# Holding back the loads of the key weights in a fused attention and MLP kernel until an earlier load has landed

## The chip, the cores and the metric

The kernel runs on one core of a Trainium2 chip. The metric is the device time of one execution in microseconds (us). The core has five instruction streams that matter here: TensorE (matrix products, PE in the profile, with its weight loads as PEld), VectorE (DVE), ScalarE (ACT), GpSimd (POOL) and SyncE (SP). SyncE, ScalarE and GpSimd also issue transfers (DMAs) between the chip's memory and the core's own memory. Issued transfers are carried out by 16 DMA engines; the profile calls SyncE's issues SPq and ScalarE's ACTq.

## The reference

One input x of 2048 tokens by 640 features goes through a linear attention block (A) and a gated MLP mixer block (B); a sigmoid gate per token mixes the two results. Only what matters for the change is shown.

```python
def _A_ref(x, wqkv, wo):
    B, S, D = x.shape              # 1, 2048, 640
    H = 32; Dh = D // H
    qkv = (x @ wqkv).reshape(B, S, 3, H, Dh).transpose(2, 0, 3, 1, 4)
    q, k, v = qkv[0], qkv[1], qkv[2]
    phi = lambda t: jnp.where(t > 0, t + 1, jnp.exp(t)) + 1e-6
    pq, pk = phi(q), phi(k)
    kv = jnp.einsum("bhsd,bhse->bhde", pk, v)
    z = jnp.einsum("bhsd->bhd", pk)
    ...
g = _sigmoid((x * gate_w).sum(-1, keepdims=True))
a = _A_ref(x, A_wqkv, A_wo)
b = _B_ref(x, B_w1, B_w2, B_w3, B_w4)
return g * a + (1 - g) * b
```

All inputs are bfloat16. The weight wqkv is 640 by 1920: columns 0 to 639 make the queries, 640 to 1279 the keys, 1280 to 1919 the values.

## The kernel before

The tokens are cut into 16 tiles of 128. x tile t is loaded as 128 rows of 640 values (160 KB) into x_tok. The products need x with features along the partitions, so each tile is also turned into xT: tiles 0 to 2 by TensorE (t_x, five transposes of 128x128 against an identity matrix, then copies by VectorE), tiles 3 to 15 by a transposing DMA (x_turn). The feature dimension of 640 is cut into five blocks k of 128. Query weights are loaded as five slices wq0 to wq4 of 128 rows by 512 columns (128 KB each) and one tail of the last 128 columns of all rows (160 KB, called wqt); key weights as five slices wk0 to wk4 of 128 rows by 640 columns (160 KB each) into wkg.

The order of work around the change is fixed by the order of the calls. The loads are issued in the order of lines 714 to 739:

| queue | order of issue |
|---|---|
| SyncE | x0, x1, wq2, x2, wk0, wk2, x3, wk4, x4, turn of x3, x5, turn of x4, tiles 6 to 9, turns of 5 to 7, tiles 10 to 15, turns of 8 to 15 |
| ScalarE | wq0, wq1, wq3, wq4, wk1, wk3, tail of wq; then the load of ScalarE's function table, and the exponentials |

A queue carries out its own instructions in order, so a wait on it holds everything behind it. Each transfer has a semaphore of its own; whoever reads its result waits for that. The helper sch.dma takes a list deps of events to wait for ahead of the issue, and keeps the event of the last transfer under each name in sch.dma_last.

TensorE begins with products on constants that only keep it busy (warmup), and then goes through q_three (line 949): the query products of token tiles 0 to 2, one per tile and block k, in a hand-written order in which the transposes of a tile are (t, None):

```python
order = [(0, 0), (1, None), (0, 1), (1, 0), (1, 1), (0, 2), (1, 2), (0, 3), (1, 3), (2, None), (0, 4), (1, 4),
         (2, 0), (2, 1), (2, 2), (2, 3), (2, 4)]
```

The transposes of tile 0 precede it. So the transposes of x tile 2 stand behind (1, 3), and the first product behind them, (0, 4), reads wq4. Then k_two (line 958) makes the key products of tiles 0 and 1, each a pair of 512 and 130 columns (line 942 and line 614 of the helper mm_kept), in this order:

```python
stream([(0, 0), (0, 1), (1, 0), (0, 2), (1, 1), (0, 3), (1, 2), (0, 4), (1, 3), (1, 4)], wkg, 130, k_out)
```

so wk0 is read first, wk1 second, wk2 fourth, wk3 sixth and wk4 eighth. The key products of tile 2 follow (k_tile, line 819), then for each further tile the query products (q_tile, line 920, helper line 606) and the key products; tile 3 is the first that reads a turned xT from a DMA. phi (line 809) turns each product into the attention's feature: an exponential on ScalarE (line 682) and two operations on VectorE. Everything later (the Gram matrix of keys and x, the MLP, the output) follows on TensorE with no change of order.

The order of the later items is chosen at build time by a list scheduler (_Items.run) with a cost model; the loads of lines 714 to 739 are issued ahead of it.

Of the kernel before, what the change touches and what calls it, by code (L numbers as in the profile page):

```python
# [11 lines left out]
D = 640  # L12
# [404 lines left out]
def _build(nc, A_x, A_wqkv, A_wo, B_w1, B_w2, B_w3, B_w4, gate_w, out, dbg=None, stop=None):  # L417
    sch = _Sched(nc)
# [80 lines left out]
    wkg = ra.alloc("wkg", [128, KD, NK], BF16)  # L499
# [206 lines left out]
        sch.dma(queue, wq[:, k, 0:512], A_wqkv[128 * k:128 * (k + 1), 0:512], "wq%d" % k)  # L706

    def load_wk(k, queue):
        sch.dma(queue, wkg[:, k, 0:D], A_wqkv[128 * k:128 * (k + 1), D:2 * D], "wk%d" % k)

    def x_turn(t):
        sch.dma("sp", xT[:, :, 128 * t:128 * (t + 1)], x_tok[:, t, :], "trx%d" % (t % 4), transpose=True)
# [9 lines left out]
    load_x(2)  # L722
    load_wq(4, "act")
    load_wk(0, "sp")
    load_wk(1, "act")
    load_wk(2, "sp")
    load_x(3)
    load_wk(3, "act")
# [241 lines left out]
    for i in range(3, NT + 2):  # L970
        if i < NT:
            addA(("q", i), 1.08, lambda t=i: q_tile(t))
            addA(("k", i), 1.36, lambda t=i: k_tile(t))
            if i % 4 == 3:
                addA(("qx", i // 4), 1.08, lambda c=i // 4: q_turned(c))
                IT.add("QB", ("qb", i // 4), 0.0, lambda c=i // 4: q_back(c),
                       deps=[(("qx", i // 4), 2.5), (("t1", NT - 1), 0.0) if i == NT - 1 else (("k", i + 1), 0.0)])
# [380 lines left out]
    for c in range(NCH):  # L1358
        for j in range(KD):
            deps = [(("t1", u), 0.9) for u in range(4 * c, 4 * c + 4)] if j == 0 else []  # L1360
# [7 lines left out]
    for t in range(NT):  # L1368
        c = t // 4
        deps = [(("w1", c, KD - 1), GEL)]  # L1370
# [8 lines left out]
    for u in range(NT):  # L1379
        deps = [(("s2", u // 4), 3.2 + 0.9 * (u % 4))]  # L1380
# [8 lines left out]
    for c in range(NCH):  # L1389
        for j in range(KFF):  # L1390
            deps = []
# [4 lines left out]
            if j == 0:  # L1396
                deps = deps0 + [(("t2", u), 0.9) for u in range(4 * c, 4 * c + 4)]
# [11 lines left out]
    for t in range(NT):  # L1409
        deps = [(("zb",), 1.0), (("q", max(t, 2)), 2.0), (("sg", 1), 0.0)]  # L1410
# [13 lines left out]
    for t in range(NT):  # L1424
# [3 lines left out]
        deps = [(("qt", t), 3.0), (("w4load",), 0.0), (("mt",), 2.5)]  # L1428
# [71 lines left out]
```

## Time and profile before

| | us |
|---|---|
| median of 3 runs | 259.19 |
| lowest and highest run | 259.15, 259.87 |
| span of the profiled execution, first to last instruction | 258.4 |
| mean granted clock of TensorE | 1.000 of full speed |
| first issue of a load (x0, on SyncE) | 0.79 |
| first exponential on ScalarE | 8.71 |

In the profile a row of the timeline has the start in us, the length in us, the engine, the line of the kernel, the operation, what it writes and reads, its shape and how many were merged; in brackets stands how long the engine was idle before it and what ended that. Products on TensorE are pipelined: a busy time of several products can hold gaps between them. The list of DMA issues gives for each group the size and the median time from the issue to the landing; asked for a window that holds one issue, it gives that one transfer's time. The q rows give what each DMA queue moved in a window, in packets, MB and as a share of 16 engines. The table by stages gives for each stretch the busy time of each engine, the granted clock, the busy share of the DMA engines and the rate in GB/s.

### The profile page before, as it was taken

How to read it: one execution, taken by the hardware profiler on the slowest of the kernel's cores; microseconds unless marked ns; L12 is line 12 of the kernel's file. 1: busy time of each engine (PE TensorE's matmuls, PEld its weight loads, DVE VectorE, ACT ScalarE, POOL GpSimd, SP SyncE). 2: the span in 40 equal slices, each digit the busy share in tenths (PEclk: the TensorE clock that was granted, in tenths of full speed). 3: DMA queues.
4: the chain of work that ended last, by engine and by line, in shares of the span. 5: the costliest groups of instructions: out<-in, count | busy, mean ns of one | idle time of the engine just before them, and what ended most of it. 6: DMA issues, size and time to landing. Idle time of an engine off the chain costs nothing.

```text
span 258.4 us, 3579 instructions
## 1 busy us (share of the span) xinstructions
PE 253.2 (98%) x1392; PEld 110.9 (43%) x1242; DVE 145.6 (56%) x290; ACT 107.0 (41%) x219; POOL 90.2 (35%) x146
## 2 busy tenths in 40 slices
PE   8899999999999999999999999999999999999997
PEld 4333333344444333334444444444444444444444
DVE  2588888899962995489999803759200033200033
ACT  1396776751356757665655600003520100253000
POOL 5012299967772143758918001223000022300000
DMA  6777799555843599462565400032100032200002
GB/s 189 221 176 182 155 142 220 157 125 119 111 102 72 103 321 387 95 103 51 127 104 128 102 10 20 0 127 50 28 0 0 20 23 101 101 1 3 0 20 102
DMA packets 57825, 26.48 MB, mean 103 GB/s; under 512 B 49188, under 2 KB 56397, under 8 KB 57808
## 3 DMA queue, kind: packets, MB, share of 16 engines
q1 hardware_dynamic: 54976, 21.87, 36.1%
q0 software_dynamic: 1168, 3.28, 4.9%
q10 hardware_dynamic: 1664, 1.11, 1.4%
q8 instruction: 10, 0.16, 0.3%
q14 instruction: 7, 0.06, 0.1%
HBM read 12.04 MB, written 2.62 MB: 57 GB/s over the span
## 4 chain that ended last, share of the span: by engine, by line
PE 95%; DMA 2%; issue 1%; SPq 0%; DVE 0%
PE ps L606 37%; PE ps L1237 30%; PE ps L625 13%; PE ps L831 7%; PE ps L614 4%; DMA x_tok<-in_A_x_dram 2%; PE ps L942 1%; PE ps L1283 1%; PE ps L1143 1%; SPq L285 0%; PE ps L1029 0%; DVE Mt L691 0%; PE ps L637 0%; PE ps L1055 0%; DVE x_tok L665 0%
## 5 line engine op out<-in xcount | busy, mean ns | idle before, releaser
L606 PE MATMUL ps<-xnT,w 128*128 128x512 bf16 x352 | 79.9, 379 | 0.5 <-issue 0.2
L665 DVE SCALAR_TENSOR_TENSOR x_tok<-ps,stg,abx 128x512 bf16<-128x512 f32 (+2 forms) x17 | 12.2, 719 | 78.4 <-PE ps L1237 78.3
L682 ACT ACTIVATE h2T<-ps 128x512 bf16<-128x512 f32 x52 | 30.7, 596 | 59.8 <-PE ps L606 59.8
L606 PEld LDWEIGHTS ps<-xnT,w 128*128 128x128 bf16 x360 | 34.6, 98 | 41.5 <-issue 2.1
L1237 PE MATMUL ps<-w,h2T 128*128 128x512 bf16 (+2 forms) x218 | 45.9, 366 | 0.3 <-issue 0.2
L648 POOL TENSOR_SCALAR xn<-x_tok,st 128x640 bf16<-128x640 bf16 x32 | 34.2, 1076 | 25.8 <-DMA xnT<-xn 25.3
L648 POOL TENSOR_SCALAR abx<-x_tok,stg 128x640 f32<-128x640 bf16 (+1 forms) x16 | 14.8, 934 | 72.1 <-DVE x_tok L665 72.1
L1237 PEld LDWEIGHTS ps<-w,h2T 128*128 128x128 bf16 x221 | 21.1, 98 | 24.2 <-issue 0.3
L682 ACT ACTIVATE Er<-ps 128x512 bf16<-128x512 f32 (+1 forms) x36 | 23.0, 648 | 15.5 <-PE ps L614 10.6
L681 ACT ACTIVATE junk<-x_tok 128x640 bf16<-128x640 bf16 x32 | 23.6, 738 | 3.9 <-DVE x_tok L663 3.7
L682 ACT ACTIVATE hsT<-ps 128x512 bf16<-128x512 f32 (+1 forms) x32 | 19.0, 593 | 13.5 <-PE ps L606 13.2
L625 PE MATMUL ps<-w,hsT 128*128 128x512 bf16 x76 | 22.3, 379 | 0.0
L625 PE MATMUL ps<-wkg,xT 128*128 128x512 bf16 x67 | 20.1, 379 | 0.1
L663 DVE SCALAR_TENSOR_TENSOR x_tok<-ps,x_tok 128x640 bf16<-128x640 f32 x16 | 13.1, 820 | 10.8 <-PE ps L614 10.2
L1237 PE MATMUL ps<-M_sb,pqnT 128*128 128x512 bf16 (+2 forms) x83 | 18.7, 366 | 0.1
L614 PE MATMUL ps<-wkg,xT 128*128 128x130 bf16 x80 | 17.6, 220 | 0.2
L831 PE MATMUL ps<-pk_tok,x_tok 128*128 128x512 bf16 x79 | 17.7, 379 | 0.1
L614 PE MATMUL ps<-w,hsT 128*128 128x128 bf16 x80 | 17.5, 219 | 0.2
L1172 DVE TENSOR_TENSOR pq_tok<-pq_tok,dnr 128x300 bf16<-128x300 bf16 (+1 forms) x48 | 17.1, 410 | 0.6
L648 DVE TENSOR_SCALAR Er<-Er 128x512 bf16<-128x512 bf16 (+1 forms) x36 | 12.2, 340 | 6.8 <-ACT Er L682 6.0
L606 PE MATMUL ps<-wq,xT 128*128 128x512 bf16 x64 | 15.9, 379 | 0.0
L656 DVE TENSOR_TENSOR qprod<-qprod,pk_tok 128x640 f32<-128x640 f32 x13 | 15.1, 1164 | 0.4
(90 smaller groups left out, 252.8 us busy)
## 6 DMA issues: line engine op xcount, KB each, us to landing
w<-in_B_w_dram SPq DMA_DIRECT2D x1, 2160.0 KB, 8.1
w<-in_B_w_dram SPq DMA_DIRECT2D x1, 2080.0 KB, 13.0
out_dram<-x_tok SPq DMA_DIRECT2D x3, 640.0 KB, 3.1
w<-in_B_w_dram POOLq DMA_DIRECT2D x8, 160.0 KB, 4.0
x_tok<-in_A_x_dram SPq DMA_DIRECT2D x6, 160.0 KB, 4.4
x_tok<-in_A_x_dram SPq DMA_DIRECT2D x1, 960.0 KB, 5.8
wv<-in_A_wqkv_dram POOLq DMA_DIRECT2D x1, 800.0 KB, 5.5
x_tok<-in_A_x_dram SPq DMA_DIRECT2D x1, 640.0 KB, 4.9
```

Source lines behind the costliest of these rows:

```text
L606: ins = e.matmul(out_ap, l, r, start=(i == 0), stop=(i == n - 1))
L614: return e.add_instruction(mybir.InstMatmult(name=nc.get_next_instruction_name(), engine=e.engine, ins=[e.lower_ap(r), ll], outs=[e.lower_ ...
L625: e.matmul(outs[0], l, r, start=st, stop=sp, skip_group_check=True)
L648: return engf(lambda e: e.tensor_scalar(out_ap, in_ap, s1, s2, op0, op1), rd, [out_ap], cost=cost)
L656: return engf(lambda e: e.tensor_tensor(out_ap, a, b_, op), [a, b_], [out_ap], cost=cost)
L663: return dve(lambda e: e.scalar_tensor_tensor(out_ap, in0, scalar, in1, op0, op1, accum_out=accum), rd, [out_ap, accum], cost=cost + 70.0)
L665: return dve(lambda e: e.scalar_tensor_tensor(out_ap, in0, scalar, in1, op0, op1), rd, [out_ap], cost=cost)
L681: return act(lambda e: e.activation(out_ap, in_ap, func, bias=bias, scale=scale, accum_out=accum), rd, wr, cost=cost)
L682: return act(lambda e: e.activation(out_ap, in_ap, func, bias=bias, scale=scale), rd, wr, cost=cost)
L831: ins = e.matmul(o, l, r, start=(t0 + q_ == 0), stop=(t0 + q_ == NT - 1))
L1172: dve(lambda e, o=o, i0=i0, i1=i1: e.tensor_tensor(o, i0, i1, ALU.mult), [i0, dnr[:, 1, sd, :]], [o], cost=cost)
L1237: ins = e.matmul(o, l, r, start=first and i == 0, stop=last and i == len(prs) - 1, skip_group_check=True)
```

## The change

Every key slice's issue gets a dependency: on SyncE's queue the event of x1, on ScalarE's the event of wq1. A queue waits once, ahead of its first key slice (wk0 on SyncE, wk1 on ScalarE); its later key slices find the event passed. What stands behind on the queue follows the wait: on SyncE wk2, x3, wk4, x4 and the turns, on ScalarE wk3, the tail of wq and the load of the function table. No other instruction is added or removed, and the order on every engine stays.

```diff
     def load_wk(k, queue):
-        sch.dma(queue, wkg[:, k, 0:D], A_wqkv[128 * k:128 * (k + 1), D:2 * D], "wk%d" % k)
+        sch.dma(queue, wkg[:, k, 0:D], A_wqkv[128 * k:128 * (k + 1), D:2 * D], "wk%d" % k,
+                deps=[sch.dma_last["x1" if queue == "sp" else "wq1"]])
```

## The prediction

> **What bounds the kernel now.** First the page's head, its busy times and its chain of what ended last:
>
> ```profile
> span 258.4 us, 3579 instructions
> ...
> PE 253.2 (98%) x1392; PEld 110.9 (43%) x1242; DVE 145.6 (56%) x290; ACT 107.0 (41%) x219; POOL 90.2 (35%) x146
> ...
> PE 95%; DMA 2%; issue 1%; SPq 0%; DVE 0%
> ```
>
> TensorE is busy for 253.2 of 258.4 us, and 95% of the chain is its own work. An edit to the loads counts only through the 5.2 us in which TensorE is idle. So the next view is the chain of waits in the first 12 us, the only stretch where a load stands in it:
>
> ```profile
> 1.26 0.41 SPq L285
> ...
> 2.18 5.75 DMA x_tok<-in_A_x_dram
> ...
> 7.98 0.45 PE ps L637 x5
> ...
> 8.44 1.82 PE ps L942 x8
> ```
>
> Columns are start, length and what. The load of x tile 2, issued at 2.18, is on the path until it lands at 7.93; from the transposes of that tile on, every step is TensorE. Time saved or lost before some 14 us therefore passes whole to the end, unless another wait appears. Next the timeline of TensorE there (two views, products and weight loads):
>
> ```profile
> 5.21 2.04 PE L942 MATMUL ps<-wq,xT 128*128 128x512 bf16 x7
> 7.98 0.45 PE L637 MATMUL ps<-ident,x_tok 128*128 128x128 bf16 x5 [0.73 <-DMA x_tok<-in_A_x_dram]
> ...
> 8.30 1.74 PE L942 MATMUL ps<-wq,xT 128*128 128x512 bf16 x7
> 9.88 0.38 PE L942 MATMUL ps<-wkg,xT 128*128 128x512 bf16 x1
> ...
> 10.15 0.38 PE L942 MATMUL ps<-wkg,xT 128*128 128x512 bf16 x1
> ```
>
> ```profile
> 6.21 0.55 PEld L942 LDWEIGHTS ps<-wq,xT 128*128 128x128 bf16 x4 [0.36 <-DMA wq<-in_A_wqkv_dram]
> ```
>
> Two waits for loads: 0.36 us for wq slice 2, then 0.73 us for x tile 2. Together 1.09 us is all that earlier loads can return. The key products start at 9.88 and follow each other every 0.27 us.
>
> **What the change moves.** No instruction is added, removed or reordered on TensorE, VectorE or GpSimd; SyncE and ScalarE each get one wait ahead of their first key slice. Their queues now:
>
> ```profile
> 2.18 0.43 SPq L285 DMA_DIRECT2D x_tok<-in_A_x_dram  x1
> 2.66 0.91 SPq L285 DMA_DIRECT2D wkg<-in_A_wqkv_dram  x2
> 3.61 0.43 SPq L285 DMA_DIRECT2D x_tok<-in_A_x_dram  x1
> 4.08 0.65 SPq L285 DMA_DIRECT2D wkg<-in_A_wqkv_dram  x1
> 4.78 0.69 SPq L285 DMA_DIRECT2D x_tok<-in_A_x_dram  x1
> 10.20 1.29 SPq L281 DMA_TRANSPOSE xT<-x_tok  x1
> ```
>
> ```profile
> 0.80 1.85 ACTq L285 DMA_DIRECT2D wq<-in_A_wqkv_dram  x4
> 2.69 0.94 ACTq L285 DMA_DIRECT2D wkg<-in_A_wqkv_dram  x2
> 3.66 0.46 ACTq L285 DMA_DIRECT2D wq<-in_A_wqkv_dram  x1
> 4.15 1.28 ACT L682 ACT_TABLE_LOAD   x1 [4.15 <-issue]
> 8.71 1.08 ACT L682 ACTIVATE Er<-ps 128x512 bf16<-128x512 f32 x2 [3.28 <-PE ps L942]
> ```
>
> And the time from issue to landing (last column, us), from the list of DMA issues asked for short windows, in this order: x1, wq1, x2, wq4, wk0, wk1, x3, wk4, and last x5, which is issued at 11.54, after all those in this list have landed:
>
> ```profile
> x_tok<-in_A_x_dram SPq DMA_DIRECT2D x1, 160.0 KB, 3.1
> ...
> wq<-in_A_wqkv_dram ACTq DMA_DIRECT2D x1, 128.0 KB, 3.3
> ...
> x_tok<-in_A_x_dram SPq DMA_DIRECT2D x1, 160.0 KB, 5.8
> ...
> wq<-in_A_wqkv_dram ACTq DMA_DIRECT2D x1, 128.0 KB, 5.9
> ...
> wkg<-in_A_wqkv_dram SPq DMA_DIRECT2D x1, 160.0 KB, 6.0
> ...
> wkg<-in_A_wqkv_dram ACTq DMA_DIRECT2D x1, 160.0 KB, 6.2
> ...
> x_tok<-in_A_x_dram SPq DMA_DIRECT2D x1, 160.0 KB, 6.6
> ...
> wkg<-in_A_wqkv_dram SPq DMA_DIRECT2D x1, 160.0 KB, 6.7
> ...
> x_tok<-in_A_x_dram SPq DMA_DIRECT2D x1, 160.0 KB, 2.6
> ```
>
> *SyncE's hold.* x1 lands at 1.26 + 3.1 = 4.36. The hand-over from a landing to a waiting queue is under 0.05 us: x3 lands at 3.61 + 6.6 = 10.2, and the transpose that waits for it starts at 10.20. So wk0 is issued at about 4.4 in place of 2.66, and what is queued behind it (wk2, x3, wk4, x4) shifts by the same 1.75 us, x4's issue ending at 5.47 + 1.75 = 7.2. Then the queue stands still until 10.20 as it does now: 3.0 us of cover.
>
> *ScalarE's hold.* The second of four issues in 1.85 us starts at 0.80 + 0.46 = 1.26; wq1 lands at about 4.6. So wk1 moves from 2.69 to 4.6, by 1.9 us, with wk3, the tail of wq and the table load behind it. The table load then runs from 6.05 to 7.35, ahead of the first exponential at 8.71: 1.35 us of cover, and without that cover it would delay the first exponential only.
>
> *Whether the key slices land later.* Were the queue ahead of them empty, wk0 would land 2.6 us (x5's time) after 4.4, at 7.0, and wk1 at 7.2. Now they land at 2.66 + 6.0 = 8.66 and 2.69 + 6.2 = 8.9. For wk4 the same sum gives 5.83 + 2.6 = 8.4 against 4.08 + 6.7 = 10.8 now, for x3 5.36 + 2.6 = 8.0 against 10.2. Every held transfer is thus issued at least 1.6 us before issuing could limit it: what sets its landing is the work queued ahead. Bounds: 0 at the best, and at the worst every landing moves by the whole shift, priced among the rivals. I take 0, the end that x5's row is nearer to.
>
> *Whether x2 and wq4 land sooner.* The reverse question: did the key slices take anything from them? The two queues' totals from 0 to 6 us (packets, MB, share of 16 engines):
>
> ```profile
> q1 hardware_dynamic: 544, 0.59, 33.1%
> q10 hardware_dynamic: 514, 0.47, 25.5%
> ```
>
> q1 is SyncE's queue, q10 ScalarE's. x0, x1, wq2 and x2 are 608 KB (0.62 MB), the four wq slices of ScalarE 512 KB (0.52 MB). Six microseconds in, neither queue had moved even that much: over the mean of the engines no key slice had begun to flow, though they had been issued for over 3 us. Landings come in the order of issue on each queue. A transfer that waits its turn behind x2 takes nothing from x2. I take 0 gain; the bound is 0.73 + 0.36 = 1.09 us. If x2 alone came sooner, little would follow: wq4, issued at 0.80 + 3 x 0.46 = 2.2, lands at 8.1, and the first product behind the transposes, which reads it, starts at 8.30, so 0.2 us is the most.
>
> *The sum.* 258.4 (span) + 0 (SyncE's hold) + 0 (ScalarE's hold) + 0 (key slices) - 0 (x2 and wq4) = 258.4 us. The runs' median, 259.19, is 0.8 above the profiled span, so 259.2 us.
>
> **The rivals.** *Gain: the queued transfers slow the ones ahead of them.* The DMA rate by stage (last column GB/s, beside it the busy share):
>
> ```profile
> 4.00:6.00 2.00, 2.00 (x14) 1.13 (x12) 1.36 (x5) 1.28 (x1) 0.71 (x5) 1.00 0.77 230
> 6.00:8.00 2.00, 1.20 (x6) 0.33 (x6) 0.00 (x0) 0.00 (x0) 0.00 (x0) 1.00 1.05 368
> ```
>
> Between 4 and 6 us, with wq2, wq3, x2 and wq4 due, the engines are 77% busy and move 230 GB/s, later 368. If the issuing and queueing of eight more transfers causes that dip, holding them lifts it: the 460 KB of that stage at 368 GB/s take 1.25 us, so x2 lands 0.75 us sooner, at 7.18, and wq4 at 7.35. The transposes then start when the products before them end, at 5.21 + 2.04 = 7.25, 0.73 us sooner; with wq2's wait gone too, up to 1.09. Time: about 258.4. For it: the dip has no other cause in these rows, and x5 alone lands in 2.6 where x2 took 5.8. Against it: most of x2's 5.8 is its turn behind x0, x1 and wq2, and both x2 and wq4 must gain. The Trainium skill, "DMA: Bandwidth & Descriptors", section "Latency and other measured facts", says that a lighter HBM load makes the fixed part of a transfer smaller; by that rule too the time would be this rival's. The trace agrees that a lone transfer is quicker, 2.6 against 5.8, but not that load beyond the turn is the reason.
>
> *Loss: late issue shows in the key products.* If the landing times are bound to the issue after all, wk0 lands at 8.66 + 1.75 = 10.4 against 9.88 (0.53 late), wk1 at 8.9 + 1.9 = 10.8 against 10.15 (0.65), wk4 at 10.8 + 1.75 = 12.5 against the eighth key product at 9.88 + 7 x 0.27 = 11.8 (0.75). These run one behind the other, so the largest counts: 0.75 us, 259.95 us. It decides from a shift of 1.0 us on, wk4's margin. x3 would then land at 11.95 and its transpose 2.5 us later, at 14.5, inside the delayed 13.96 + 0.75 = 14.7 of the product that reads it, and adds nothing:
>
> ```profile
> xT<-x_tok SPq DMA_TRANSPOSE x1, 2.5
> ...
> 13.96 1.24 PE L606 MATMUL ps<-wq,xT 128*128 128x512 bf16 x5
> ```
>
> For it: the hold is real, 1.75 us. Against it: x5's row. The Trainium skill's rule on the same page, section "Rules for kernel authors", speaks against the change as well: issue early and wait late, so that the fixed cost is overlapped. By that rule the sum would be this rival's 259.95.
>
> *The wait holds nothing.* If x1 had landed when the queue came to the wait, all would stay at 259.2. The rows exclude it almost: the queue arrives at 2.66, x1 at 4.36.
>
> **How the numbers follow.** No change 0.56 (own range 258.9 to 259.5); gain 0.24, of which I put 0.16 beyond 0.78 us, since that needs wq2's wait too or a still larger lift; loss 0.18, of which 0.13 beyond 0.78, its price of 0.75 standing at that edge and any wait that I have not seen adding to it; the idle wait 0.02. With 0.3% (0.78 us) as about what a measurement of this kernel can tell from no change: faster 0.16, same 0.71, slower 0.13. The range 258.3 to 260.0 takes in the gain up to 0.9 us and the loss up to 0.8, and leaves out the last 0.2 us of the gain's bound and losses past the priced one: under 2 in 10.
>
> **What would show it.** Right: wk0's issue at 4.4 and wk1's at 4.6, the table load ended before 7.5, x2's landing within 0.2 us of 7.93, wk4's within 0.5 us of 10.8, TensorE's wait for x tile 2 still near 0.7 and no wait for wkg. The gain: x2 and wq4 landing near 7.2, the transposes at 7.25, a rate near 368 GB/s already between 4 and 6 us. The loss: a TensorE or weight-load wait for wkg around 10 to 12 us. I am wrong if the two queues do not keep the order of issue, or if the rate after 6 us falls because the held transfers are issued only then.

## The result and the profile after

| | before | changed |
|---|---|---|
| median of 22 runs each, us | 259.08 | 259.72 |
| lowest and highest run, us | 258.18, 260.11 | 258.57, 260.41 |
| span of the profiled execution, us | 258.4 | 258.6 |

The ratio of the changed kernel to the one before is 1.0022, with a 95% interval of 1.0012 to 1.0032: 0.6 us slower, real, but under the 0.3% that the prediction takes for no change. The forecast was 259.2 us in a range of 258.3 to 260.0. The measured time lies in that range, 0.5 us above the forecast, outside the 258.9 to 259.5 that belonged to no change, and nearer to the 259.95 of the rival for the loss. That it is this near is luck: things that the forecast had put at nothing have opposite signs and nearly the same size. The page of the changed kernel, its head, busy times and the chain of what ended last by engine:

```profile
span 258.6 us, 3605 instructions
...
PE 254.8 (99%) x1418; PEld 111.0 (43%) x1242; DVE 146.3 (57%) x290; ACT 107.1 (41%) x219; POOL 90.3 (35%) x146
...
PE 91%; DMA 7%; SPq 1%; DVE 0%; issue 0%
```

Two things are to be seen. TensorE's count went from 1392 to 1418 although the change adds no product: records of products can be missing from a trace, so neither count nor busy time is compared. And transfers, which held 2% of the chain, hold 7%. The chain of the changed kernel, from its start, tells which (start, length, what):

```profile
1.25 2.92 DMA x_tok<-in_A_x_dram
...
4.19 0.33 SPq L285
...
5.04 5.54 DMA x_tok<-in_A_x_dram
...
10.59 1.29 SPq L281
...
11.93 2.66 DMA x_tok<-in_A_x_dram
...
14.61 6.26 DMA xT<-x_tok
...
20.91 1.25 PE ps L606 x5
```

Before, the chain left the loads at 7.98 us, with the transposes of x tile 2, and was TensorE from there on. Now it runs through SyncE's queue up to 20.91: x1's landing releases the held queue (4.19), x3 is loaded (5.04 to 10.58), then turned, then x5 lands, and the turn of tile 5, issued at 14.61, lands only 6.26 us later. The query products of tile 5 wait for it. TensorE's timeline there, changed kernel (products; then the weight load of the transposes of tile 2, before and changed; then products again):

```profile
5.21 1.86 PE L943 MATMUL ps<-wq,xT 128*128 128x512 bf16 x7
6.91 0.44 PE L637 MATMUL ps<-ident,x_tok 128*128 128x128 bf16 x5
...
8.79 0.38 PE L943 MATMUL ps<-wkg,xT 128*128 128x512 bf16 x1
...
9.47 0.39 PE L943 MATMUL ps<-wkg,xT 128*128 128x512 bf16 x1 [0.24 <-DMA wkg<-in_A_wqkv_dram]
```

```profile
7.98 0.28 PEld L637 LDWEIGHTS ps<-ident,x_tok 128*128 128x128 bf16 x5 [1.22 <-DMA x_tok<-in_A_x_dram]
```

```profile
6.84 0.33 PEld L637 LDWEIGHTS ps<-ident,x_tok 128*128 128x128 bf16 x5 [0.27 <-DMA x_tok<-in_A_x_dram]
```

```profile
13.35 1.24 PE L606 MATMUL ps<-wq,xT 128*128 128x512 bf16 x5
...
20.91 1.25 PE L606 MATMUL ps<-wq,xT 128*128 128x512 bf16 x5 [0.62 <-DMA xT<-x_tok]
```

The products no longer stand idle for x tile 2, and the weight loads wait less: 0.27 us for x tile 2 in place of 1.22, 0.18 us for wq slice 2 in place of 0.36. The transposes of tile 2 start at 6.91 in place of 7.98, the key products at 8.79 in place of 9.88. The second key product, which reads wk1, then waits for its load. The query products of tile 3 start at 13.35 against 13.96, and those of tile 5 at 20.91 against 20.74: the lead is used up between tiles 3 and 5. The two held queues and some of their landings (the last column is us from issue to landing; in order x2, wq4, wk0, wk1, wk4, turn of tile 5):

```profile
4.19 0.80 SPq L285 DMA_DIRECT2D wkg<-in_A_wqkv_dram  x2
...
14.61 1.21 SPq L281 DMA_TRANSPOSE xT<-x_tok  x1
```

```profile
4.49 0.85 ACTq L285 DMA_DIRECT2D wkg<-in_A_wqkv_dram  x2
...
5.86 1.28 ACT L682 ACT_TABLE_LOAD   x1 [5.86 <-issue]
7.63 1.08 ACT L682 ACTIVATE Er<-ps 128x512 bf16<-128x512 f32 x2 [0.48 <-PE ps L943]
```

```profile
x_tok<-in_A_x_dram SPq DMA_DIRECT2D x1, 160.0 KB, 4.6
...
wq<-in_A_wqkv_dram ACTq DMA_DIRECT2D x1, 128.0 KB, 4.8
...
wkg<-in_A_wqkv_dram SPq DMA_DIRECT2D x1, 160.0 KB, 3.9
...
wkg<-in_A_wqkv_dram ACTq DMA_DIRECT2D x1, 160.0 KB, 4.9
...
wkg<-in_A_wqkv_dram SPq DMA_DIRECT2D x1, 160.0 KB, 5.6
...
xT<-x_tok SPq DMA_TRANSPOSE x1, 6.3
```

x2 took 5.8 before and takes 4.6, wq4 5.9 and now 4.8. The first exponential still waits for TensorE, not for the table load that ends ahead of it. The table by stages (busy time of PE, PEld, DVE, ACT and POOL with their counts, granted clock, busy share of the DMA engines, GB/s) shows the dip between 4 and 6 us, 230 GB/s before, at 292, and between 6 and 8 us 282, where it was 368:

```profile
4.00:6.00 2.00, 2.00 (x14) 1.11 (x12) 1.36 (x5) 0.14 (x1) 0.73 (x5) 1.00 0.98 292
6.00:8.00 2.00, 2.00 (x15) 0.97 (x15) 0.58 (x4) 1.52 (x2) 0.00 (x0) 1.00 0.88 282
```

One thing about the profile before has to be known for all that follows: x2 came late in it. Two further profiles of the same kernel (under the experiments) have spans of 257.8 us in place of 258.4. In all runs where time and span are of the same execution, the time is 1.2 to 1.3 us above the span; the 0.8 of the prediction compared one execution's span with the median of others.

### The profile page after: what moved, and what is told of

The parts are those of the page before. It is cut to its first block, busy times and chain, and to the rows that moved or that the text cites. A ratio compares the mean times of both kernels' runs of the same rounds, so it can differ in the third digit from the quotient of the medians.

```text
span 258.6 us, 3605 instructions
## 1 busy us (share of the span) xinstructions
PE 254.8 (99%) x1418; PEld 111.0 (43%) x1242; DVE 146.3 (57%) x290; ACT 107.1 (41%) x219; POOL 90.3 (35%) x146
## 4 chain that ended last, share of the span: by engine, by line
PE 91%; DMA 7%; SPq 1%; DVE 0%; issue 0%
PE ps L606 36%; PE ps L1238 30%; PE ps L625 12%; PE ps L832 7%; DMA x_tok<-in_A_x_dram 4%; PE ps L614 3%; DMA xT<-x_tok 2%; PE ps L1284 1%; PE ps L1144 1%; SPq L281 0%; SPq L285 0%; PE ps L1030 0%; DVE Mt L691 0%; PE ps L1056 0%; DVE x_tok L665 0%
## 5 line engine op out<-in xcount | busy, mean ns | idle before, releaser
L625 PE MATMUL ps<-w,hsT 128*128 128x512 bf16 x80 | 23.0, 379 | 0.0
```

The costliest lines, as they stand in the source:

```text
L625: e.matmul(outs[0], l, r, start=st, stop=sp, skip_group_check=True)
```

## The experiments

Every row of the table is one execution. Columns: time from issue to landing of x2 and of wq4, start of the key products, of tile 3's and of tile 5's query products, issue of the turn of tile 5, and its time to landing, all in us.

| kernel | x2 | wq4 | keys | tile 3 | tile 5 | turn of 5 | to land | span |
|---|---|---|---|---|---|---|---|---|
| before | 5.8 | 5.9 | 9.88 | 13.96 | 20.74 | 14.15 | 4.9 | 258.4 |
| before (e5) | 4.6 | 5.6 | 9.35 | 13.44 | 20.21 | 14.00 | 5.2 | 257.8 |
| before (e6) | 5.1 | 5.3 | 9.33 | 13.42 | 20.19 | 13.54 | 5.0 | 257.8 |
| changed | 4.6 | 4.8 | 8.79 | 13.35 | 20.91 | 14.61 | 6.3 | 258.6 |
| changed (e1) | 4.4 | 4.5 | 9.08 | 13.29 | 21.07 | 14.47 | 6.6 | 258.7 |
| changed (e10) | 4.0 | 4.2 | 8.49 | 12.96 | 20.44 | 13.96 | 6.4 | 258.1 |
| changed (e11) | 3.8 | 3.9 | 9.06 | 13.15 | 19.92 | 13.38 | 4.7 | 257.5 |
| e4, ScalarE's hold alone | 4.9 | 5.1 | 9.53 | 13.61 | 20.39 | 12.70 | 4.9 | 258.0 |
| e9, SyncE's hold alone | 5.6 | 5.7 | 9.73 | 13.82 | 20.59 | 14.46 | 4.9 | 258.2 |
| e2, changed and reordered | 4.3 | 4.5 | 8.64 | 13.58 | 20.36 | 13.22 | 2.5 | 258.0 |
| e12, changed, x5 earlier | 4.2 | 4.3 | 8.84 | 13.48 | 20.25 | 13.73 | 5.2 | 257.9 |
| e3, before and reordered | 4.8 | 5.0 | 8.92 | 13.01 | 19.79 | 11.99 | 2.5 | 257.4 |
| e7, x3 ahead of the hold | 4.8 | 5.1 | 9.10 | 14.21 | 20.98 | 14.46 | 4.9 | 258.6 |
| e8, hold until x2 and wq4 | 4.6 | 4.7 | 9.46 | 14.65 | 21.43 | 15.36 | 5.1 | 259.1 |

In each of the 14, the span less the start of tile 5's products is 237.6 us. So whatever sets one execution apart from another has happened by then.

### e1, the changed kernel once more

No edit.

> The changed kernel once more. In the first profile of it the query products of tiles 0 to 2 came 1.07 us sooner (x2 and wq4 landed 1.1 us sooner), 0.4 us went back to wk1, and all the rest and 0.8 us more went to the query product of tile 5, which waited for the turned tile 5 until 20.9 us. Theory A (the turn of tile 5 lands late in every execution, because the transfers behind the hold come 0.4 us later on SyncE's queue): the wait at 20 to 21 us is there again, 0.5 us or more, and the ratio to the kernel before is 1.001 to 1.003. Rival B (that wait was an accident of one execution and the loss in the timed runs comes from the key slices): no wait for the turned tile 5, the key products later than 9.9 us instead.

Median of 5 runs 259.74 us, 1.0031 (1.0019 to 1.0043) of the kernel before. The late turn is there again, and longer. TensorE's timeline of e1:

```profile
21.07 1.25 PE L606 MATMUL ps<-wq,xT 128*128 128x512 bf16 x5 [0.83 <-DMA xT<-x_tok]
```

The loss at tile 5 is no accident of one execution; that it comes in every execution, as theory A has it, is refuted by e11 below.

### e2 and e3, the turn of tile 5 earlier, with and without the hold

The load of x5 is issued ahead of the turn of tile 3, and the turn of tile 5 ahead of the load of tiles 6 to 9: e2 in the changed kernel, e3 in the one before.

```diff
     load_x(4)
+    load_x(5)
     x_turn(3)
-    load_x(5)
...
     x_turn(4)
-    for t0, t1, turns in ((6, 10, range(5, 8)), (10, NT, range(8, NT))):
+    x_turn(5)
+    for t0, t1, turns in ((6, 10, range(6, 8)), (10, NT, range(8, NT))):
```

> The changed kernel with the load of x5 issued ahead of the turn of tile 3 and the turn of tile 5 ahead of the load of tiles 6 to 9. Theory A: the turn of tile 5 is issued near 13.2 in place of 14.6 and lands before 17, no wait at tile 5; TensorE keeps its 0.6 us, so the ratio to the kernel before is about 0.9975 (0.996 to 0.999), unless the load of tiles 6 to 9, now 0.65 us later, makes tile 6 wait. Rival B: nothing returns, ratio 1.001 to 1.003 as without the reordering.

> The kernel before with the same reordering and no hold: the control. TensorE does not wait for tile 5 in the kernel before, so theory A says that it returns nothing: ratio 0.999 to 1.001. If the reordering alone is worth as much as in the changed kernel, the ratio is 0.997 and what it returns there has nothing to do with the hold.

e2: 258.96 us, 1.0003 (0.9991 to 1.0015). e3, the control: 259.15 us, 1.0006 (0.9992 to 1.0019). The turn lands 2.5 us after its issue in both, and in e2 nothing waits for it:

```profile
20.36 1.24 PE L606 MATMUL ps<-wq,xT 128*128 128x512 bf16 x5
```

So the slowdown of the changed kernel goes away when the turn of tile 5 is taken out of its late place, and the same move gives the kernel before nothing that can be told. That places the loss at this turn. But the ratio of 0.9975 that theory A gave for e2 was missed; e2 doesn't beat the kernel before: its key products start at 8.64, then wait for a key slice, and tile 3 starts only at 13.58:

```profile
PE ps L943 <- DMA wkg<-in_A_wqkv_dram: 0.5, 1, 0.5
```

### e4 and e9, each hold alone

```diff
-                deps=[sch.dma_last["x1" if queue == "sp" else "wq1"]])
+                deps=[sch.dma_last["wq1"]] if queue == "act" else [])      # e4
+                deps=[sch.dma_last["x1"]] if queue == "sp" else [])        # e9
```

> The hold on ScalarE's queue alone (wk1, wk3, the tail of wq and the table load after wq1); SyncE's queue as before. If the dip in the transfer rate between 4 and 6 us comes from the table load on ScalarE (4.15 to 5.43 before), x2 lands near 6.8 and wq4 near 7.0 as in the changed kernel. If it comes from the issuing of the eight later transfers, half of them held gives about half: x2 near 7.4. If it comes from the transfers queued behind on the same queue only, wq4 gains and x2 stays at 7.9. By theory A the time is then the kernel before's or less (0.997 to 1.000), since x3 is not held and the turn of tile 5 stays where it was.

> The hold on SyncE's queue alone. Two further looks at the kernel before gave 257.8 us with the key products starting at 9.3 to 9.4; the first profile of it (258.4, key products at 9.88) was slow with x2. Against those, the changed kernel's TensorE is 0.1 us ahead after the key products of tiles 0 and 1 and then loses 0.8 us to the turn of tile 5, and the hold on ScalarE alone cost nothing clear of noise. Theory A (the loss comes through SyncE's queue: x3 and x4 late, so the turn of tile 5 late): x3 lands near 10.5, the turn of tile 5 is issued near 14.5, tile 5 waits, ratio 1.002 to 1.003. Rival B (the loss comes through the key slices of both queues): no wait at tile 5, a wait for wk0 or wk2 of 0.5 us or more.

e4: 259.24 us, 1.0009 (0.9996 to 1.0021). e9: 258.99 us, 1.0004 (0.9991 to 1.0017). ScalarE's hold costs nothing that these runs can tell, though e4's interval also reaches into that of the changed kernel. On the three causes that e4 was to tell apart it doesn't decide: x2 lands at 7.12 and wq4 at 7.34, between the values foreseen, and the kernel before alone scatters from 6.80 to 7.93 and from 7.49 to 8.12. e9 is a miss for the theory that SyncE's hold makes the loss through its own chain: the turn of tile 5 is issued as late as in the changed kernel (14.46), but lands 4.9 us later, and its row shows it:

```profile
xT<-x_tok SPq DMA_TRANSPOSE x1, 4.9
```

TensorE doesn't wait there: the turn lands at 19.41, 1.2 us ahead of the products of tile 5 (20.59). It would have been in time for the changed kernel too, whose tile 5 would start at 13.35 + 6.77 = 20.12 without a wait. So the late issue alone costs nothing; what costs is the long landing. Neither hold alone has brought x2 and wq4 forward by as much as the two together (5.6 and 5.7, 4.9 and 5.1, against 3.8 to 4.6 and 3.9 to 4.8).

### e5, e6, e10 and e11, two more profiles of each kernel

No edit: e5 and e6 are the kernel before, e10 and e11 the changed one.

> The kernel before, looked at again. Theory C (the hold does not make x2 land sooner; the first profile of the kernel before caught an execution in which one DMA engine was late with x2): x2 lands near 7.0, not 7.93, and the transposes of tile 2 start near 7.0 as in the changed kernel, without any hold. Rival D (the hold is what brings x2 forward by 1.1 us): x2 lands near 7.9 again and the transposes start near 8.0.

> A third look at the kernel before, as the one ahead of it. Theory C: transposes of tile 2 near 7.0, or anywhere between 6.9 and 8.0 with no fixed value. Rival D: near 8.0.

> The changed kernel, third profile. In two of two the turn of tile 5 took 6.3 and 6.6 us to land in place of 4.9 to 5.2: its last two completion packets came 1 us after the others, just as a 16 KB instruction fetch of 1 us ended. Theory A: 6 us or more again and a wait of 0.6 to 0.9 us at tile 5 at about 21 us, or, if the meeting with the fetch depends on tenths of a microsecond, 4.9 to 5.2 us, no wait at tile 5 and a span of about 257.8. A span of 258.6 without a wait at tile 5 would speak against it.

> The changed kernel, fourth profile; as the third. The timed runs of the changed kernel lie in two clumps, 258.6 to 259.4 and 259.7 to 260.4, so a meeting with the fetch in somewhat over half of the executions is expected.

One run each: 259.09, 259.08, 259.34 and 258.84 us. TensorE's timeline of e5, then of e6:

```profile
7.00 0.44 PE L637 MATMUL ps<-ident,x_tok 128*128 128x128 bf16 x5
...
9.35 0.38 PE L942 MATMUL ps<-wkg,xT 128*128 128x512 bf16 x1
```

```profile
7.44 0.44 PE L637 MATMUL ps<-ident,x_tok 128*128 128x128 bf16 x5
...
9.33 0.38 PE L942 MATMUL ps<-wkg,xT 128*128 128x512 bf16 x1
```

The products don't wait for x tile 2, and the weight load ahead of the transposes waits only 0.2 us for it. In e5 x2 lands at 6.80 and the transposes start at 7.00 without any hold, as theory C expected; in e6 it is 7.28 and 7.44. What held TensorE in these is a slice of wq, and less of it (waits of e5, then of e6):

```profile
PE ps L942 <- DMA wq<-in_A_wqkv_dram: 0.4, 1, 0.4
```

```profile
PE ps L942 <- DMA wq<-in_A_wqkv_dram: 0.3, 1, 0.3
```

So the 0.73 us that the prediction put in the balance for x2 were one execution's. The key products of e5 start at 9.35 all the same, because wq4 lands only at 7.78. In the trace of the kernel before, 15 of the 16 engines had done their share of x2 by 7.00 us, and the last at 7.93. Of the two of the changed kernel, e10 has the late turn and e11 has not (timelines of e10 and of e11):

```profile
20.44 1.25 PE L606 MATMUL ps<-wq,xT 128*128 128x512 bf16 x5 [0.54 <-DMA xT<-x_tok]
```

```profile
13.15 1.24 PE L606 MATMUL ps<-wq,xT 128*128 128x512 bf16 x5
...
19.92 1.24 PE L606 MATMUL ps<-wq,xT 128*128 128x512 bf16 x5
```

In e11, tile 5 follows tile 3 by 6.77 us, as in the kernel before (6.77 and 6.78), and the span is 257.5, under all three profiles of the kernel before. Where the turn is late, tile 5 follows by 7.56, 7.78 and 7.48: 0.7 to 1.0 us lost.

### e7, x3 ahead of the hold

`load_x(3)` is moved from behind wk2 to ahead of wk0, so that it isn't held.

```diff
+    load_x(3)
     load_wk(0, "sp")
...
     load_wk(2, "sp")
-    load_x(3)
```

> The changed kernel with the load of x3 issued ahead of the hold on SyncE's queue, so that only the key slices and x4 wait. Theory A (the time goes to the turn of tile 5, which comes late because x3 and x4 do): x3 lands near 8, the turn of tile 3 starts near 8.2 in place of 10.5, the turn of tile 5 is issued only when x5 has landed, at about 12.5 to 13.5, and lands by 18.5; no wait at tile 5, ratio to the kernel before 0.998 to 1.001. Rival B (the loss is in the key slices): wk0 and wk2 come behind x3 and are later still, ratio 1.002 to 1.004 with a wait for a key slice of 0.5 us or more.

259.72 us, 1.0017 (1.0005 to 1.003): no better than the changed kernel, and a miss for theory A. It is no clean test of it, though: the turn of tile 5 is issued at 14.46, as late as in the changed kernel, because x4, still held, lands at 12.58. The turn lands in 4.9. But wk2, which is put behind 160 KB more, lands at 10.87, and TensorE waits for it, as rival B expected (waits of e7):

```profile
PE ps L942 <- DMA wkg<-in_A_wqkv_dram: 0.8, 1, 0.8
```

### e8, the hold until x2 and wq4

```diff
-                deps=[sch.dma_last["x1" if queue == "sp" else "wq1"]])
+                deps=[sch.dma_last["x2" if queue == "sp" else "wq4"]])
```

> A longer hold: the key slices wait for x2 (SyncE) and wq4 (ScalarE), near 7.0. The prediction gave 1.0 us as the margin of the landing of the key slices; here nothing is queued ahead of them any more, so the issue sets their landing: wk0 at about 7.0 + 2.6 = 9.6, wk4 near 11.5 to 12. Expected: TensorE waits for key slices, 0.5 to 1.5 us in all, the turn of tile 5 comes still later, and the ratio is 1.004 to 1.010. If the key slices' lateness costs nothing even here, the ratio stays at the changed kernel's 1.002 to 1.003.

260.41 us, 1.0064 (1.0041 to 1.0087). wk0 is issued at 6.80. The DMA engines run dry behind x2 (stages of e8), and TensorE waits twice for key slices (waits of e8):

```profile
6.00:8.00 2.00, 1.89 (x13) 0.92 (x14) 0.50 (x3) 0.00 (x0) 0.00 (x0) 1.00 0.20 28
```

```profile
PE ps L942 <- DMA wkg<-in_A_wqkv_dram: 1.2, 2, 0.8
```

So late issue can show in the key products, as the prediction's rival for the loss said; with the hold at x1 about a third of its price shows (0.25 of 0.75 us, the mean of four profiles, worked out below).

### e12, only the load of x5 earlier

As e2, but only `load_x(5)` goes ahead of the turn of tile 3; the turn of tile 5 stays behind the load of tiles 6 to 9.

```diff
     load_x(4)
+    load_x(5)
     x_turn(3)
-    load_x(5)
```

> The changed kernel with only the load of x5 moved ahead of the turn of tile 3; the load of tiles 6 to 9 still stands ahead of the turn of tile 5. SyncE's chain behind x3 gets 0.6 to 1.0 us shorter: the turn of tile 5 is issued near 13.8 in place of 14.6 and lands by 19.5 even if it takes 5.2 us, or by 20.4 at 6.6 us. Theory A: the wait at tile 5 is gone or at most 0.3 us, ratio 0.999 to 1.001. Rival B: ratio 1.002 to 1.003 unchanged.

259.14 us, 1.0002 (0.9988 to 1.0016). The turn takes the usual 5.2 us and nothing waits for it. That takes the loss away without moving the turn past the big load, so its place behind the big load alone doesn't make the loss. It doesn't show that the turn can no longer be late: landing at 18.89, it would hold up the products of tile 5 (20.25) by only 0.1 us if it came 1.5 us later.

## Why the prediction came out as it did

*The sum.* From the profiles, four of the changed kernel and three of the one before, as means:

| step | changed against before, us |
|---|---|
| start of the key products, 8.86 against 9.52 | -0.66 |
| from there to tile 3, 4.33 against 4.09 | +0.25 |
| from tile 3 to tile 5, 7.40 against 6.77 | +0.62 |
| from tile 5 to the end | 0 |
| together | +0.2 |

In e1 the first key product itself waits for wk0, so the gain ahead of it and what key slices take back are each a little larger than these means. The forecast had 0 in each of these. The timed difference is 0.6 us over 22 runs, 0.4 more than the profiles' +0.2. The sample accounts for it: less 1.25 us outside the span, the medians stand for spans of 257.8 and 258.5, while the profiled spans have means of 258.0 and 258.2. The profiles are thus 0.2 us slower than the typical run of the kernel before and 0.3 faster than that of the changed one, and the sizes in the table are no better than that.

*x2 and wq4 land no sooner: wrong.* This is the first step that failed: "A transfer that waits its turn behind x2 takes nothing from x2." In the changed kernel x2 lands 3.8 to 4.6 us after its issue, before 4.6 to 5.8 (means 4.2 and 5.2); wq4 3.9 to 4.8 against 5.3 to 5.9 (means 4.35 and 5.6). The eight executions with both queues held have 3.8 to 4.8 and 3.9 to 5.1, the four with none held 4.6 to 5.8 and 5.0 to 5.9. The step rested on the totals of the two queues, which are means over 16 engines. The landings of the single engines' shares tell more: five slices have 80 shares, and of these 35 had landed before the last share of x2 in the trace before, 3 in e5, 32 in e6 and 16 in e3, but 10, 6, 0 and 0 in the four of the changed kernel. Key slices did flow on some engines while others were still at x2. That this is what slows x2 isn't shown; the trace doesn't name the engine of a share.

The rival for the gain had the sign of this step right, and its 0.73 us is near the 0.66 that the profiles give before anything is paid back, though it was priced from a trace that itself was 0.5 us late there. Not all of the 0.66 is the hold's: e3 starts its key products at 8.92 without any hold, and e10 and e11 differ by 0.57 us there although in neither do the products wait for a load. In e11 the seven query products ahead of the transposes of tile 2 take 2.05 us, in e10 1.77. The rival's cause, a dip in the rate that the held transfers make, isn't borne out: between 4 and 6 us the rate is 292 to 307 GB/s in the four of the changed kernel and 230, 273 and 339 in the three before, so the scatter between executions is as wide as the effect. The dip also had another candidate in the prediction's own rows, ScalarE's table load from 4.15 to 5.43. The Trainium skill, "DMA: Bandwidth & Descriptors", section "Latency and other measured facts", says that lighter load on the memory lowers the fixed part of a transfer; these rates don't show a lighter load while x2 was under way, so the gain of x2 can't be put down to that rule here.

*Key slices land no later: right by the clock, wrong by the need.* In the means the five slices land between 0.1 us sooner and 0.3 us later than before (wk4 at 10.8 in both). But the products that read them now come 0.66 us earlier, and the slices don't. One sign that the prediction named for being wrong did come: after 6 us the rate falls, because the held slices are issued only at 4.2 to 5.7. Between 6 and 8 us it is 269 to 284 GB/s in the four of the changed kernel against 335 to 368 in the three before. "No wait for wkg" failed: in the profile of the changed kernel the products are idle 0.24 us for wk1, and from the first key product to tile 3 they take 4.56 us in place of 4.08. Over the four the excess is 0 to 0.5, in the mean 0.25. The prediction set each margin against the old start of the key products, and didn't ask what the margins are once the gain is there.

*ScalarE's hold 0: right.* The table load ends at 7.14, the first exponential starts at 7.63 and waits for TensorE; e4 shows no cost that can be told from none.

*SyncE's hold 0, with 3.0 us of cover: right for the shift, wrong for what follows on the queue.* wk0 was issued at 4.19 to 4.4 as worked out. The cover was taken to the turn of tile 3, and there the step stopped; the rival for the loss said of x3 that it "adds nothing". Two tiles on, the turn of tile 5 is issued at 14.1 in the mean against 13.9, while TensorE is 0.4 us ahead at tile 3. That shift alone would cost nothing: with the 5.2 us that it takes at most elsewhere, the turn would land at 19.81 in the changed kernel, for products that would start at 20.12. But in 3 of the 4 profiles of the changed kernel the turn lands after 6.3 to 6.6 us; in the nine other executions in which it stands behind the load of tiles 6 to 9 (e11 is one) it lands after 4.7 to 5.2. So the step took the landing time of a later transfer for given, and that is what changed. e1, e2 and e12 show that the loss is there and that it goes when the turn doesn't land late.

*What makes it land late.* The trace records when each of the 16 DMA engines has done its share of a transfer. For the load of tiles 6 to 9, which stands right ahead of the turn of tile 5 on SyncE's queue, for that turn, and for the one instruction fetch of 16 KB that falls near them (us):

```
             fetch            last share   turn of tile 5:
             start   length   of load 6-9  15th share   16th share
before       18.21   1.16     18.26        18.90        19.00
e5 (before)  18.42   1.16     18.46        19.14        19.16
e6 (before)  17.78   1.16     17.82        18.50        18.50
e11          17.35   1.16     17.39        18.06        18.07
e12          18.09   1.16     18.14        18.77        18.89
e9           18.69   1.16     18.73        19.41        19.41
e4           16.83   1.16     16.87        17.52        17.63
e7           18.60   1.16     18.64        19.32        19.32
e8           19.75   1.16     19.80        20.47        20.49
changed      18.86   0.97     18.68        19.30        20.87
e1           19.00   0.98     18.87        19.54        21.02
e10          18.38   0.97     18.26        18.90        20.39
```

In the three late ones 15 engines are done at the usual time, 0.6 to 0.7 us behind the load of tiles 6 to 9, and one engine is 1.5 us late. There the fetch begins after that load is done (by 0.12 to 0.18 us), in all nine others 0.04 to 0.05 before. What the queues moved in the changed kernel, in three windows, from 18.85 to 18.9, from 18.9 to 19.75 and from 19.75 to 20 us:

```profile
q8 instruction: 1, 0.02, 121.0%
```

```profile
DMA packets 0, 0.00 MB, mean 0 GB/s; under 512 B 0, under 2 KB 0, under 8 KB 0
```

```profile
q1 hardware_dynamic: 83, 0.02, 35.6%
```

The fetch starts, then for 0.85 us no packet starts anywhere, and only at its end (18.86 + 0.97 = 19.83) do the last two packets of SyncE's queue ahead of the next turn come (19.81 and 19.82). They are the last of 32 packets of 4 bytes with which the turn ends, two for each engine if they are shared evenly. In all twelve executions the last of them starts behind the fetch's start: by 0.96 to 1.04 us in the three late ones, by 0.21 to 0.23 in the nine others. That the fetch holds up one engine's last packets of the turn is read from its place in time, in three late executions out of three; no run moved the fetch alone, so it is not shown by experiment. The Trainium skill, "DMA: Bandwidth & Descriptors", section "Queues, rings and completion order", says that an engine goes round its queues packet by packet and that its semaphore increment lands only after all its earlier writes; one late share out of 16 agrees with it.

Why the fetch begins late just there stays open, and whose instructions it brings isn't shown. Its start keeps to the end of the load in all twelve, which moves from 16.87 (e4) to 19.80 (e8); so it isn't free of the queues itself. Whether the turn lands late goes with how far TensorE is ahead of SyncE's queue: taking the issue of the turn of tile 5 less the start of tile 3's products, the three late ones have 1.00, 1.18 and 1.26 us, all others 0.71 (e8) or less. Both halves of the change push that way: TensorE comes sooner, and SyncE's chain a little later. That is a relation in 14 executions, not a shown cause. No version tried is faster than the kernel before: e2, e3, e4, e9 and e12 come out level with it.

## What to carry to other kernels

Earlier work in front of an engine is worth only what every later input of that engine can match: after a gain, work out each margin again from the new, earlier start, and follow the moved queue to its later readers, here two tiles beyond the place where the prediction stopped. Before a wait in a profile is priced, take a second execution of the same kernel; 0.73 us of wait for x tile 2 stood in one profile of three. And where a sum of zeros comes out right, ask whether the terms are zero or cancel.

## What was not expected of the hardware

Where one instruction fetch of 16 KB, about 1 us long, begins behind the end of the load of tiles 6 to 9 and not just ahead of it, one engine of 16 is 1.5 us late with the turn of tile 5, and the whole transfer with it: 6.3 to 6.6 us in place of 4.7 to 5.2. And the landing of the same 160 KB, x2, issued at the same time with the same work ahead of it, scattered between 4.6 and 5.8 us in three executions of the same kernel, a spread as wide as the whole effect that was looked for.
